# Two chunks of a normalised input, transposed by DMA on ScalarE's queue instead of by TensorE

## The chip, the cores and the metric

One Trainium2 chip; the kernel runs on one core. The metric is the device time in microseconds of one execution, lower is better. Each version is run several times and the median is taken; one further execution is profiled, and its trace gives the durations below.

## The reference

A layer normalisation of `x` (2048 rows of 1024) feeds two branches that are multiplied: a sliding, dilated attention (32 heads of 32, 8 keys at a stride of 2) and a gated MLP of width 3584. Everything is bfloat16 at the surface.

```python
xn  = layernorm(x)                           # over the 1024 columns
qkv = xn @ wqkv                              # 1024 -> 3 x 1024
o   = softmax(q . k[pos - 2*w], w = 0..7) v  # keys before row 0 masked
s   = o @ wo
g   = silu((silu(xn @ w1) * (xn @ w3)) @ w2)
out = x + s * g
```

## The kernel before, in words

**Tiling.** The 2048 rows are four chunks of 512 (`CH`), worked through as two blocks (`b` = 0, 1) of two chunks each; a chunk is four blocks of 128 rows (`NST`). The products with `wqkv`, `w1`, `w3`, `w2` and `wo` are done by a Strassen-like scheme with seven instead of eight half products: sums of weights and of activations are formed on VectorE (DVE), and TensorE multiplies them.

**What is transposed.** TensorE needs `xn` with its 1024 columns on the partitions. `xT` holds two chunks in that form (`half` = chunk mod 2, eight column groups of 128). For every 128-row block, `ln_tp` (L420) does it on TensorE: eight matmuls with the identity (L429) into two PSUM banks, and two ScalarE copies (L436) from there to `xT`. Chunks 0 and 1 are done at the start. Chunks 2 and 3 are done in `mlp_down(0)`, the second matrix product of the MLP for block 0.

**The stage around the change.** `mlp_down` runs seven products for each of four row groups `g`, one product being 14 matmuls of 128x512: w (0,0), w (1,0), T2, T1, w (1,1), T3, T4 in this order. Their right sides are loaded by SP in two halves of 896 KB each, from the weight (`w`) or from prepared sums in DRAM (`t_dram`). The left side of T1 is a sum `s1` which VectorE has put into `xT`'s memory, since the old `xT` is not needed any more; so a row group's part of `xT` comes free as its T1 product ends (cells `s1_cells`, `xt_cells`). During the first products the new x of chunks 2 and 3 is loaded into two buffers of the pool `r8` (r_5 and r_0 in the trace's numbering) and normalised in place on ScalarE (`ln_act`; its last step is L416, done before 297 us).

The T1 product goes to the banks `de`; ScalarE copies them to float32 tiles (`dsp`), and the w (1,1) product then goes on in the same banks. VectorE adds T3 and the `dsp` copies (`dsa`), and ScalarE makes the SiLUs (`gsilu`). In T3 and T4 each row group starts with an `ln_tp` of one block of chunk 2 or 3.

**What follows.** `wo(0)`, with loads of `wo` (two halves of 1 MB) and of `x` through SP; then block 1, whose attention of chunk 1 (`attention(1)`, on VectorE) and q, k, v products read `xT` and the sums `xs` of it (`xn_sums`: xs0, xs1, xs2, and later xs3).

**Order.** Nothing is issued directly: `plan.op` records every operation with what it reads and writes, a cost, and for transfers a size. TensorE's order is that of the program. For the other four engines a small simulation (`simulate`) picks, whenever an engine is free, the ready operation with the earliest due time. So a changed operation can shift the order on VectorE, ScalarE, SP and GpSimd, and the choice of buffers. All operations of one kind are emitted from one line: L307 matmuls, L316 VectorE's tensor operations, L321 ScalarE copies, L324 SiLUs, L330 DMA issues.

Of the kernel before, what the change touches and what calls it, by code (L numbers as in the profile page):

```python
# [14 lines left out]
PE, DVE, ACT, POOL, SP = range(5)  # L15
# [184 lines left out]
def kernel(  # L200
# [11 lines left out]
    nc = tc.nc  # L212
    P = 128
# [45 lines left out]
    xT = const.tile([P, 2, KT, CH], BF16, name="xT")  # L259
# [5 lines left out]
    plan = Plan()  # L265
# [13 lines left out]
        out=ident[:], in_=ident[:], compare_op=ALU.not_equal, fill=1.0,  # L279
# [4 lines left out]
        out=maskb[0:32], in_=maskb[0:32], compare_op=ALU.is_ge, fill=-1.0e9,  # L284
# [12 lines left out]
    def bank(name):  # L297
        return plan.slot("mm", name)
# [15 lines left out]
    def tt(name, fn, o, a, b, rd, wr, n, fast, late=0.0):  # L314
        occ = n / (1920.0 if fast else 960.0) + 0.068
        plan.op(DVE, name, lambda: fn(out=o(), in0=a(), in1=b()), rd, wr, occ, 0.08, late=late)  # L316
# [19 lines left out]
    def xt_cells(half, kh, st=None):  # L336
        return [("xT", half, (kh * KH + k) * 2 + q // 2, q % 2) for k in range(KH)
                for q in (range(4) if st is None else [st])]
# [17 lines left out]
    def f32(s):  # L356
        return s.ap()
# [17 lines left out]
    def xrow(xt, st):  # L375
        return xt.ap().rearrange("p (s d) -> p s d", s=NST)[:, st, :]
# [43 lines left out]
    def ln_tp(c, st, xt, engs=(ACT, ACT)):  # L420
        half = c % 2
        for kh in range(2):
            eng = engs[kh]
            tp = bank(f"tp{c}_{st}_{kh}")

            def emit(kh=kh, tp=tp):
                for k in range(KH):
                    kt = kh * KH + k
                    nc.tensor.matmul(  # L429
                        tp.ap()[:, k * P:(k + 1) * P], lhsT=xrow(xt, st)[:, kt * P:(kt + 1) * P], rhs=ident[:],  # L430
                        start=(k == 0), stop=(k == KH - 1), skip_group_check=True,
                    )

            plan.op(PE, f"tp{c}_{st}", emit, [(xt, st)], [tp], KH * TP, 0.0)
            fn = nc.scalar.copy if eng == ACT else nc.vector.tensor_copy
            plan.op(eng, f"xT{c}_{st}_{kh}", lambda kh=kh, tp=tp, fn=fn: fn(  # L436
                out=xT[:, half, kh * KH:(kh + 1) * KH, st * P:(st + 1) * P],
                in_=tp.ap().rearrange("p (k t) -> p k t", k=KH)),
                [tp], xt_cells(half, kh, st), 0.48 if eng == ACT else 0.6, 0.11, late=-1.5 if c == 1 else 0.0)


    def qkv_load(t):
# [400 lines left out]
    def gsilu(c, dh, g, src, rd, occ):  # L843
        dst, wr = gate(c, dh, g)
        silu("dg", dst, src, rd, wr, occ)

    def mlp_down(b):
# [20 lines left out]
        def prod(ps, g, row, fh, rhs, first, dt):  # L868
            src = h_sb if dt == BF16 else h16
            for q, (wt, ops) in enumerate(rhs):  # L870
                fs = range(fh * FH + q * NQ, fh * FH + (q + 1) * NQ)
                mm(ps, [lambda f=f: src[:, f, gs[row][g]] for f in fs], ops, first and q == 0,
                   [wt] + h_cells(fs, row, [g]), last=q == 1)
# [9 lines left out]
        xn = []  # L883
        for c in range(2 * b + 2, 2 * b + 4 if b + 1 < NB else 0):
            xt = plan.slot("r8", f"x{c}")
# [43 lines left out]
        rhs = rhs_load("t", t=T3)  # L929
        for g in G:  # L930
            if b + 1 < NB:
                ln_tp(2 * b + 2, g, xn[0])
            prod(pb[g], g, 1, 0, rhs, False, FP16)
            tt("dsa", add, lambda g=g: f32(sp5[g]), pb[g].ap, lambda g=g: f32(sp5[g]), [pb[g], sp5[g]], [sp5[g]], 512, False)
            gsilu(2 * b + 1, 1, g, lambda g=g: f32(sp5[g]), [sp5[g]], 0.54)
        rhs = rhs_load("t", t=T4)
        for g in G:
            if b + 1 < NB:
                ln_tp(2 * b + 3, g, xn[1])
            prod(pb[g], g, 1, 1, rhs, False, BF16)  # L940
            gsilu(2 * b + 1, 0, g, pb[g].ap, [pb[g]], 0.48)

# [142 lines left out]
    def rows0(st):  # L1085
        if st == 0:
            for q in range(2):
                ln_tp(0, q, x0)
        elif st < NST - 1:
            ln_tp(0, st + 1, x0, (ACT, ACT))  # L1090

    plan.shift = 0.0
    for b in range(NB):
# [50 lines left out]
        for fb in range(FB):  # L1144
            up_step(b, fb)
        attention(c0)
        mlp_down(b)
        wots = wo_load()
        wo_sums(wots)
# [35 lines left out]
```

## Time and profile before

| | us |
|---|---|
| median of 3 runs (lowest to highest) | 728.78 (727.29 to 729.50) |
| the profiled execution | 729.82 |
| its span | 728.1 |
| TensorE busy | 716.1 |
| VectorE busy | 643.0 |
| ScalarE busy | 394.4 |
| identity matmuls (L429), 128 in all | 219 ns median each, overlapping; 64 of them at 319 to 344 us |
| granted TensorE clock, mean | 0.995 of full |

The span is the time from the first to the last instruction on the core; the profiled execution's own time has some 1.7 us around it. Busy times of different engines overlap. Matmuls are pipelined, so the durations of single ones overlap too; the chain of work that ended last gives each piece without overlap. `mm`, `r`, `k`, `a` in the profile's rows are the pools of PSUM banks, of 8 KB buffers, of float32 tiles and of attention tiles.

### The profile page before, as it was taken

What the parts mean: (1) busy time and instruction counts of PE and PEld (TensorE: products, weight loads), DVE (VectorE), ACT (ScalarE), POOL (GpSimd) and SP (SyncE); (2) the same over time, 40 slices, a digit from 0 to 9 for tenths busy, and PEclk for the clock granted to TensorE, in tenths of its full rate; (3) what the DMA queues carried; (4) which work ended last, traced back from release to release, by engine and by line L of the source; (5) the groups of instructions that cost most, each with busy time, mean ns of one, the idle gap of its engine ahead of it and who ended that gap; (6) DMA issues with size and microseconds to landing.
All of it is one profiled execution on the core that took longest, in us unless ns stands there. A gap on an engine that the chain in (4) does not pass through costs nothing.

```text
span 728.1 us, 9409 instructions
## 1 busy us (share of the span) xinstructions
PE 716.1 (98%) x3436; PEld 348.4 (48%) x3436; DVE 643.0 (88%) x860; ACT 394.4 (54%) x672; POOL 50.0 (7%) x102
## 2 busy tenths in 40 slices
PE   7999999999999999999999999999999999999997
PEld 5555544444444444445455554444444444444443
DVE  5898999987999999764999999965999998959957
ACT  6745465657565698454444454666555654411233
POOL 0010110112000000202000000022000002020000
PEclk9999999999999999999999999999999999999999
DMA  9569886786544844477355549897537346473523
GB/s 322 199 214 382 319 298 203 256 234 224 185 170 145 302 143 162 149 212 231 117 174 174 172 150 309 280 298 238 190 115 248 117 153 210 153 252 109 174 72 102
DMA packets 120142, 148.47 MB, mean 204 GB/s; under 512 B 5408, under 2 KB 97056, under 8 KB 115744
## 3 DMA queue, kind: packets, MB, share of 16 engines
q1 hardware_dynamic: 114016, 121.65, 52.0%
q0 software_dynamic: 6080, 26.22, 9.7%
q8 instruction: 27, 0.44, 0.3%
q14 instruction: 19, 0.16, 0.1%
HBM read 106.95 MB, written 32.51 MB: 192 GB/s over the span
## 4 chain that ended last, share of the span: by engine, by line
PE 90%; DVE 5%; DMA 3%; ACT 0%; SPq 0%; issue 0%; DVEq 0%
PE mm L307 89%; DVE r L316 2%; DMA h_sb<-in_B_w_dram 2%; DMA r<-in_A_wqkv_dram 1%; DVE h_sb L316 1%; PE mm L429 1%; DVE xs L316 1%; DVE qo L316 1%; DVE small L384 0%; ACT h_sb L321 0%; SPq L330 0%; DVE r L392 0%; ACT qo L321 0%; DVE small L391 0%; DVE small L387 0%
## 5 line engine op out<-in xcount | busy, mean ns | idle before, releaser
L307 PEld LDWEIGHTS <-r 128*128 128x128 f16 (+1 forms) x2288 | 240.5, 107 | 245.3 <-DVE r L316 0.9
L307 PE MATMUL mm<-xs,r 128*128 128x512 f16 x1280 | 295.4, 379 | 0.8 <-DVE r L316 0.5
L307 PE MATMUL mm<-xT,r 128*128 128x512 bf16 (+1 forms) x1008 | 228.3, 371 | 0.5 <-DMA r<-in_A_wqkv_dram 0.5
L321 ACT COPY k<-mm 128x512 f32<-128x512 f32 x192 | 112.2, 586 | 88.2 <-PE mm L307 85.4
L307 PE MATMUL mm<-r,h_sb 128*128 128x512 bf16 (+1 forms) x704 | 154.9, 379 | 0.0
L307 PEld LDWEIGHTS <-h_sb 128*128 128x128 f16 (+1 forms) x800 | 77.9, 98 | 92.5
L321 ACT COPY mm<-mm 128x512 f32<-128x512 f32 x88 | 50.3, 573 | 83.9 <-PE mm L307 69.9
L316 DVE TENSOR_TENSOR a<-a,a 128x2048 bf16<-128x2048 bf16 (+1 forms) x72 | 87.7, 1218 | 1.3 <-DMA a<-E 0.9
L316 DVE TENSOR_TENSOR a<-qo,kT 128x2048 bf16<-128x2048 bf16 x64 | 76.8, 1217 | 0.0
L316 DVE TENSOR_TENSOR k<-mm,k 128x512 f32<-128x512 f32 x72 | 47.9, 684 | 22.0 <-PE mm L307 21.6
L316 DVE TENSOR_TENSOR a<-E,vT 128x2048 bf16<-128x2048 bf16 x56 | 66.4, 1217 | 0.0
L316 DVE TENSOR_TENSOR h_sb<-mm,k 128x512 bf16<-128x512 f32 x96 | 63.1, 683 | 1.1 <-PE mm L307 0.7
L316 DVE TENSOR_TENSOR r<-r,r 128x1024 f16<-128x1024 bf16 (+4 forms) x66 | 52.3, 798 | 7.9 <-DMA r<-in_A_wqkv_dram 5.9
L324 ACT ACTIVATE k<-k 128x512 bf16<-128x512 f32 x56 | 34.8, 631 | 44.3 <-DVE k L316 44.2
L324 ACT ACTIVATE h_sb<-mm 128x512 bf16<-128x512 f32 x60 | 35.8, 598 | 20.5 <-PE mm L307 20.4
L316 DVE TENSOR_TENSOR a<-a 128x1024 bf16<-128x1024 bf16 (+4 forms) x60 | 37.9, 632 | 9.0 <-DMA a<-E 8.0
L316 DVE TENSOR_TENSOR h_sb<-h_sb,k 128x1024 bf16<-128x1024 bf16 x56 | 36.8, 684 | 9.2 <-ACT k L321 9.0
L316 DVE TENSOR_TENSOR qo<-qo,a 128x2048 bf16<-128x2048 bf16 x32 | 39.0, 1217 | 0.0
L321 ACT CAST k<-mm 128x512 bf16<-128x512 f32 x56 | 32.6, 586 | 11.5 <-PE mm L307 11.5
L330 POOL DMA_DIRECT2D a<-E x32 | 16.6, 525 | 321.7 <-ACT k L321 138.9
L316 DVE TENSOR_TENSOR h_sb<-h_sb 128x512 f16<-128x512 bf16 (+1 forms) x72 | 37.5, 567 | 0.8 <-PE mm L307 0.6
L316 DVE TENSOR_TENSOR r<-r 128x1024 f16<-128x1024 bf16 (+1 forms) x34 | 25.7, 776 | 0.0
(75 smaller groups left out, 408.5 us busy)
## 6 DMA issues: line engine op xcount, KB each, us to landing
r<-in_B_w_dram SPq DMA_DIRECT2D x42, 512.0 KB, 4.3
s_dram<-r POOLq DMA_DIRECT2D x14, 1024.0 KB, 5.6
r<-t_dram SPq DMA_DIRECT2D x16, 896.0 KB, 6.3
r<-s_dram SPq DMA_DIRECT2D x14, 1024.0 KB, 6.1
r<-in_A_wqkv_dram SPq DMA_DIRECT2D x12, 1024.0 KB, 7.4
r<-in_B_w_dram SPq DMA_DIRECT2D x12, 896.0 KB, 5.1
h_sb<-in_B_w_dram SPq DMA_DIRECT2D x14, 512.0 KB, 10.2
t_dram<-h_sb POOLq DMA_DIRECT2D x14, 512.0 KB, 6.9
```

The source lines that it names most:

```text
L307: nc.tensor.matmul(cut(ps.ap()), lhsT=lhs[k](), rhs=cut(rhs[k]()), start=(first and k == 0), stop=(last and k == n - 1), skip_group_check= ...
L316: plan.op(DVE, name, lambda: fn(out=o(), in0=a(), in1=b()), rd, wr, occ, 0.08, late=late)
L321: plan.op(ACT, name, lambda: nc.scalar.copy(out=o(), in_=a()), rd, wr, occ, 0.11)
L324: plan.op(ACT, name, lambda: nc.scalar.activation(out=o(), in_=a(), func=ACTF.Silu), rd, wr, occ, 0.11, table="silu")
L330: plan.op(eng, name, lambda: e.dma_start(out=o(), in_=a()), rd, wr, occ, 0.0, nbytes=kb * 1024, late=late)
L429: nc.tensor.matmul(tp.ap()[:, k * P:(k + 1) * P], lhsT=xrow(xt, st)[:, kt * P:(kt + 1) * P], rhs=ident[:], start=(k == 0), stop=(k == KH - ...
```

## The change

In `mlp_down(0)`, the eight calls of `ln_tp` for chunks 2 and 3 become calls of a new function `ln_turn`. It records one transfer on ScalarE's queue for each block of 128 rows: from the normalised rows (128 x 1024, bfloat16, 256 KB) straight to the block's place in `xT` (128 x 8 x 128), transposed by the DMA. Chunks 0 and 1 stay on `ln_tp`. The planner is told 1.5 us of ScalarE and 256 KB for each.

```diff
+    def ln_turn(c, st, xt):
+
+        half = c % 2
+        plan.op(ACT, f"turn{c}_{st}", lambda: nc.scalar.dma_start(
+            out=xT[:, half, :, st * P:(st + 1) * P], in_=xrow(xt, st), transpose=True),
+            [(xt, st)], xt_cells(half, 0, st) + xt_cells(half, 1, st), 1.5, 0.0, nbytes=256 * 1024)
...
         rhs = rhs_load("t", t=T3)
         for g in G:
             if b + 1 < NB:
-                ln_tp(2 * b + 2, g, xn[0])
+                ln_turn(2 * b + 2, g, xn[0])
             prod(pb[g], g, 1, 0, rhs, False, FP16)
...
         rhs = rhs_load("t", t=T4)
         for g in G:
             if b + 1 < NB:
-                ln_tp(2 * b + 3, g, xn[1])
+                ln_turn(2 * b + 3, g, xn[1])
             prod(pb[g], g, 1, 1, rhs, False, BF16)
```

In the program that the planner makes of it, the transfers stand on ScalarE behind the `dsp` copies, two after each of the four, as soon as `xT` comes free; xs0, xs1 and xs2 stand between the `dsa` sums on VectorE; and the first load of `wo`, which reuses the buffer of chunk 2, stands ahead of T4's loads on SP.

## The prediction

> **What bounds the kernel now.** I read the page first: busy time and the chain that ended last.
>
> ```profile
> PE 716.1 (98%) x3436; PEld 348.4 (48%) x3436; DVE 643.0 (88%) x860; ACT 394.4 (54%) x672; POOL 50.0 (7%) x102
> PE 90%; DVE 5%; DMA 3%; ACT 0%; SPq 0%; issue 0%; DVEq 0%
> ```
>
> TensorE sets the end. The chain in order of time shows whether the removed work lies on it:
>
> ```profile
> 319.60 0.45 PE mm L429 x8
> 320.04 3.02 PE mm L307 x14
> ...
> 343.88 0.45 PE mm L429 x8
> 344.32 35.84 PE mm L307 x166
> ```
>
> Each group of eight L429 transposes is a piece of the chain between two products of 14 matmuls. Next, TensorE's timeline over the products around the change (each of four groups: the one on T1, a w product into the same banks, T3; T4 follows):
>
> ```profile
> 295.26 12.25 PE L307 MATMUL mm<-r,xT 128*128 128x512 f16 x56
> 307.35 12.25 PE L307 MATMUL mm<-r,h_sb 128*128 128x512 bf16 x56
> 319.43 0.61 PE L429 MATMUL mm<-ident,r 128*128 128x128 bf16 x8
> 319.88 3.19 PE L307 MATMUL mm<-r,h_sb 128*128 128x512 f16 x14
> ```
>
> There is no gap, so every load and copy is in time there. Whether it stays so depends on ScalarE, where the transfers go, and on SP's queue:
>
> ```profile
> 298.48 0.59 ACT L321 COPY k<-mm 128x512 f32<-128x512 f32 x1 [1.86 <-PE mm L307]
> 301.50 0.59 ACT L321 COPY k<-mm 128x512 f32<-128x512 f32 x1
> 304.53 0.58 ACT L321 COPY k<-mm 128x512 f32<-128x512 f32 x1 [2.44 <-PE mm L307]
> 307.55 0.58 ACT L321 COPY k<-mm 128x512 f32<-128x512 f32 x1 [2.44 <-PE mm L307]
> ```
>
> ```profile
> 306.79 0.53 SPq L330 DMA_DIRECT2D r<-t_dram  x1
> 307.37 1.88 SPq L330 DMA_DIRECT2D a<-E  x3
> 309.34 0.53 SPq L330 DMA_DIRECT2D r<-t_dram  x1
> 318.12 1.88 SPq L330 DMA_DIRECT2D r<-t_dram  x2
> ```
>
> The four copies are `dsp`, one for each T1 product; the waits of 2.44 us between them are free ScalarE time. The two single `t_dram` loads are T3's halves, the pair at 318.12 is T4's. The DMA view for 299 to 317 us (40 slices of 0.45 us, busy tenths) and three of its landing rows:
>
> ```profile
> DMA  9999640000000055576589899999999999999830
> r<-t_dram SPq DMA_DIRECT2D x2, 896.0 KB, 7.4
> out_dram<-r SPq DMA_DIRECT2D x12, 256.0 KB, 2.3
> r<-in_A_x_dram SPq DMA_DIRECT2D x16, 256.0 KB, 5.3
> ```
>
> The engines fill up when T3's loads start and fall empty at about 316.2: there T3's data has landed.
>
> **What goes away.** Eight groups on the chain, 8 x 0.45 = 3.60 us of TensorE. Sixteen ScalarE copies (L436; pairs of 1.07, so 16 x 0.53 = 8.5 us) go too; ScalarE is off the chain and waits 1.6 to 1.9 us before most pairs, so that is worth nothing.
>
> **What comes in: ScalarE's issue time.** The changed program's order puts two transfers behind each `dsp` copy. The copies must be read before the second w product adds to the same bank: it starts at 307.35 and goes on by 3.02, so `dsp` 1, 2 and 3 must end by 310.4, 313.4 and 316.4. A transposing issue is in no row here. The nearest rows are SP's plain issues, 0.36 (`t_dram`) to 0.94 us (half of the pair's 1.88). I take 0.94, since the new form is the harder one, and keep an upper end open for a rival. Then the first pair leaves by 299.07 + 1.88 = 300.95, before `dsp` 1 at 301.50; the same holds for the later pairs: all eight fit in the 2.44 us gaps. `dsp` is not delayed; price nothing. Behind the last pair at about 310.0 wait the SiLUs (first at 311.36), the kT halo copy and the softmax exponential (323.07); none is late.
>
> **What comes in: waits between the queues.** In the built program, ScalarE's transfers take turns with SP's on eight completion semaphores, and each transfer waits for the one before on its semaphore. The wait lists give: T3's first half waits for the third transpose in order of issue, an `a<-E` transfer ahead of T3's second half waits for the fifth (first of chunk 3), T4's first half waits for the seventh, the second `wo` load for the eighth, and the sixth and seventh transposes themselves, on ScalarE, wait for the second and fourth. The first `wo` load, which overwrites chunk 2, moves ahead of T4's loads. T3's second half is the tightest: product T3 now begins at 319.43, and needs it after seven matmuls of 0.216, at 320.94. The fifth transpose leaves at 304.53 + 0.58 + 0.94 = 306.05. Landing: 2.3 us (`out`, 256 KB) to 5.3 us (`x`, 256 KB). I take 5.3, as this window is busy: 311.4. One 0.6 us issue and T3's load of 7.4 us give 319.4; at 2.3 us it is not later than today's 309.34. Spare: 1.5 us at worst. T3's first half: third transpose leaves at 302.1 + 0.94, lands by 308.4, load by 315.8, wanted at 319.43. T4, wanted at 331.5: seventh leaves at 309.1, lands by 314.4; T4's issue is held by TensorE until 318 anyway. Price nothing, with 1.5 us the margin.
>
> **What comes in: bytes.** 8 x 256 KB = 2.1 MB; at the 310 GB/s that the slices hold while full, 6.8 us of all 16 engines. The slices before 309 us leave 5.4 us free. The remaining 1.4 us push T3's landing from 316.2 to 317.6, still early. The far end: q1's 114,016 packets took 52% of 16 x 728.1 us, 53 ns each; a transfer cut into 1,024 pieces of 256 bytes is then 3.4 us, eight 27 us; in pieces of 32 bytes eight times that. I take the copy's speed, the rows of equal size.
>
> **DVE.** xs0, xs2 and xs1 (1.14 us each) move from 346.9-351.5 to between the T3 sums, where DVE waits up to 2.78 us at a time; they need all eight transposes, wanted near 326, landed by 316. T3 and T4 end earlier, so `wo`'s second load (9.5 us to landing, DVE's 6.74 us wait) is issued 1.8 us earlier. Together DVE is 3.4 + 1.8 us ahead, more than the 3.6 TensorE gains, so the next point at which TensorE waits for it (0.47 us at 384.08) comes no worse. What is late next is T3's second half.
>
> **Sum.** 729.82 (profiled: span 728.1 and 1.7 around it) - 3.60 = 726.2. The three runs' median, 728.78, is 1.0 below that execution, so I give 728.78 - 3.60 = 725.2. A measurement of this kernel tells 0.3% (2.2 us) from no change.
>
> **Rivals.** *The transfers are slow and TensorE waits for T3 (slower).* For it: no row shows a transpose by DMA, and queues couple. At 3.4 us each the fifth lands at 300 + 17 = 317, T3's half at 325, a wait of 4 us; queued behind everything (27 us and the 10 that these slices hold already, from 299) it would be 336, a wait of 15. Net +0.5 to +11.4, middle +6: 735. It decides from where the fifth lands after 312.9, about 2.6 us each, and loses the whole gain at 3.3. The Trainium skill speaks for it: VectorE: DVE Perf Modes, "The three transpose paths", gives a 128x128 transpose 390 ns on TensorE and 1309 ns by DMA, and says to use TensorE where PSUM will do. By that eight blocks, if one after another, are an estimated 10.5 us a transfer, and the time near 775; the row here is 0.45 us for eight blocks on TensorE, and no row shows the DMA.
>
> *The issue is long and ScalarE holds its copies (slower).* At 4 us each `dsp` 2 ends at 299.07 + 16.6 + 0.6 = 316.3 (wanted 313.4) and `dsp` 3 at 324.9: TensorE stands 8.4 us, and T3's load, behind the fifth transpose, makes it 1.2 to 4.2 more: net +6 to +9, near 736. With the tightest sum above it breaks even between 2.2 and 2.8 us, by the landing. Against it: plain issues of up to 1,024 pieces take 0.94. The Trainium skill's DMA: Bandwidth & Descriptors, in the table behind "Why a DMA increments its semaphore by 16 and not by 1", gives earlier generations 32 cycles of the issuing sequencer per tile of a transpose within SBUF; with its 512 cycles for a plain issue beside 0.366 us here, an estimated 1.5 us for 64 tiles, 2.9 for 128. By 1.5 the sum holds, by 2.9 it lies between +0.5 and +3.5.
>
> *The gain is eaten:* issues of about 2 us or landings some microseconds over 5.3 give 727 to 730. That the transposes stay on TensorE is excluded: its program has 64 matmuls fewer.
>
> **Numbers.** Forecast 0.45 (alone 724 to 727), eaten 0.12, long issue 0.23, slow transfers 0.20. So faster 0.45, same 0.12, slower 0.43. The range takes in the forecast, the eaten gain, the long issue and the nearer half of the slow transfers: 724 to 741.
>
> **What would show it.** Right: L429 gone from 319-344, the products touching, the first T3 matmul near 319.4, `dsp` copies at today's times, T3's second load issued before 313. Wrong: TensorE idle before T3 with a DMA as releaser (slow transfers), before the second w product with ScalarE as releaser (long issue), or DVE waiting at xs for transposes after 330.

## The result, and the profile after

| | us |
|---|---|
| median before (5 runs, lowest to highest) | 728.78 (727.28 to 729.54) |
| median after (5 runs, lowest to highest) | 731.90 (729.63 to 732.78) |
| ratio after / before | 1.0039 (95% interval 1.0023 to 1.0055) |
| profiled execution after, its span | 731.11, 729.3 |

The change made the kernel slower by 3.1 us; 3.6 us less had been forecast. The profiled executions differ by less, 731.11 against 729.82, because the one of before lies 1.0 above its median and the one of after 0.8 below. So the rows below account for the 1.3 us between these two executions and show by which mechanism the sign turned.

The traces here reach the start of the T1 products between 292.2 and 295.5 us. The three whose granted clock does not fall to half in the first 20 us (e1, e3 and e7 below) come at 292.2 to 293.0, the others at 293.9 to 295.5. So stages are compared from that start on (first row of the third fence below).

The page of after: the 64 identity matmuls are gone (3436 became 3372 instructions), TensorE is less busy, and yet the span is longer.

```profile
PE 714.7 (98%) x3372; PEld 345.1 (47%) x3372; DVE 642.6 (88%) x860; ACT 388.0 (53%) x656; POOL 50.0 (7%) x102
```

The chain in order of time (start, duration, what) now leaves TensorE. It goes through an attention transfer `a<-E` on SP and then through T3's second load:

```profile
306.09 8.29 DMA a<-E
...
314.44 10.42 DMA r<-t_dram
...
324.90 395.62 PE mm L307 x1825
```

TensorE's timeline (start, duration, what, and in brackets the idle time before the row with what ended it):

```profile
295.09 12.25 PE L307 MATMUL mm<-r,xT 128*128 128x512 f16 x56
307.17 12.25 PE L307 MATMUL mm<-r,h_sb 128*128 128x512 bf16 x56
320.19 1.67 PE L307 MATMUL mm<-r,h_sb 128*128 128x512 f16 x7 [0.77 <-DMA r<-t_dram]
324.90 24.37 PE L307 MATMUL mm<-r,h_sb 128*128 128x512 f16 x105 [3.04 <-DMA r<-t_dram]
349.11 1.89 PE L307 MATMUL mm<-r,qo 128*128 128x512 bf16 x8
```

T3 waits 0.77 us for its first half and 3.04 us for its second. The 105 matmuls that follow take 24.37 us; the same 105 take 22.82 us where nothing disturbs them (second row of `e2_plain_copy`, below). The table by stretch says why (start and end, length, then busy time of PE, PEld, DVE, ACT and POOL with their counts, then the granted clock, DMA share and GB/s): after the wait the clock falls to half for some 3 us.

```profile
324.00:326.00 2.00, 1.10 (x3) 0.41 (x3) 0.76 (x1) 0.00 (x0) 0.00 (x0) 0.66 1.12 196
326.00:328.00 2.00, 2.00 (x6) 0.75 (x5) 0.46 (x1) 0.00 (x0) 0.00 (x0) 0.50 1.10 351
328.00:330.00 2.00, 2.00 (x11) 0.88 (x9) 1.77 (x4) 1.10 (x2) 0.00 (x0) 0.98 1.08 346
```

ScalarE's timeline shows the `dsp` copies and behind each a pair of transposing transfers:

```profile
298.31 0.59 ACT L321 COPY k<-mm 128x512 f32<-128x512 f32 x1 [1.87 <-PE mm L307]
298.37 3.31 ACTq L444 DMA_TRANSPOSE xT<-r  x2
301.72 0.58 ACT L321 COPY k<-mm 128x512 f32<-128x512 f32 x1 [2.82 <-PE mm L307]
301.74 2.71 ACTq L444 DMA_TRANSPOSE xT<-r  x2
304.49 0.58 ACT L321 COPY k<-mm 128x512 f32<-128x512 f32 x1 [2.19 <-PE mm L307]
304.57 3.57 ACTq L444 DMA_TRANSPOSE xT<-r  x2
308.19 0.58 ACT L321 COPY k<-mm 128x512 f32<-128x512 f32 x1 [3.11 <-PE mm L307]
308.21 10.55 ACTq L444 DMA_TRANSPOSE xT<-r  x2
318.81 0.63 ACT L324 ACTIVATE h_sb<-k 128x512 bf16<-128x512 f32 x1 [10.04 <-issue]
```

The copies begin within 0.7 us of their old times. The last pair is another matter: its two issues take 4.74 and 5.72 us and hold ScalarE, so the first SiLU, which stood at 311.36 before, begins at 318.81. No wait of TensorE in these rows is put down to it. SP's queue shows T3's two loads, which stood at 306.79 and 309.34 before:

```profile
307.46 0.72 SPq L330 DMA_DIRECT2D r<-t_dram  x1
308.23 5.02 SPq L330 DMA_DIRECT2D a<-E  x3
314.44 0.37 SPq L330 DMA_DIRECT2D r<-t_dram  x1
```

Last, the DMA view for 299 to 317 us: the free slices of before (digits 0 from 302 to 305 us) are filled, and q10, the transposes, alone takes 61% of the engines' time. The shares of the queues add up to over 100%, since packets of different queues overlap on an engine. T3's halves now take 12.7 and 10.4 us to land (6.3 and 8.6 before), and even the 64 KB `a<-E` transfers 8.3 instead of 4.4.

```profile
DMA  9999969989999998999999899989997999999999
q10 hardware_dynamic: 6384, 1.59, 61.4%
r<-t_dram SPq DMA_DIRECT2D x2, 896.0 KB, 11.6
a<-E SPq DMA_DIRECT2D x8, 64.0 KB, 8.3
```

The account, up to the first `wo` product: -3.60 (identity matmuls) + 0.77 + 3.04 (waits) + 1.55 (105 matmuls at 24.37 instead of 22.82) = +1.8; that product starts at 349.11 instead of 347.18, +1.9, and counted from the start of T1 +2.1. (The products overlap: 12.25 us long, they follow each other every 12.08. So each of the two waits costs some 0.17 us more than the idle time in brackets.) Behind it, before's wait of 0.47 us at 384.08 is gone.

**Measures used below.** "Stage" is the time from the start of T1 to a product well into block 1's q, k, v (the fifth run of 16 matmuls on `xs`, at 420.37 before): 125.11 us before, 126.54 after. "Piece" is the time of one packet of q10 (some 256 bytes) on its engine: q10's share, times the window, times 16 engines, over its packets; after, in 299 to 339 us, 36.4% x 40 us x 16 / 8,448 = 27.6 ns (e9, whose transfers go out later: 322 to 350 us). Since packets overlap on an engine, a piece's time beside other transfers holds waiting too.

### The profile page after: what moved, and what is told of

Its sections match the earlier page's. It is cut to its first block, busy times and chain, and to the rows that moved or that the text cites. A ratio compares the mean times of both kernels' runs of the same rounds, so it can differ in the third digit from the quotient of the medians.

```text
span 729.3 us, 9290 instructions
## 1 busy us (share of the span) xinstructions
PE 714.7 (98%) x3372; PEld 345.1 (47%) x3372; DVE 642.6 (88%) x860; ACT 388.0 (53%) x656; POOL 50.0 (7%) x102
## 3 DMA queue, kind: packets, MB, share of 16 engines
q10 hardware_dynamic: 8448, 2.10, 2.0%
## 4 chain that ended last, share of the span: by engine, by line
PE 80%; DVE 14%; DMA 3%; issue 1%; ACT 0%; SPq 0%; DVEq 0%
PE mm L307 80%; DVE a L316 6%; DVE h_sb L316 3%; DVE r L316 2%; DMA r<-t_dram 1%; DMA a<-E 1%; DVE qo L316 1%; DMA r<-in_A_x_dram 1%; DVE k L316 1%; DVE small L384 1%; DVE xT L316 1%; PE mm L429 0%; DVE E L316 0%; SPq L330 0%; DVE r L392 0%
## 5 line engine op out<-in xcount | busy, mean ns | idle before, releaser
L324 ACT ACTIVATE k<-k 128x512 bf16<-128x512 f32 x56 | 34.8, 631 | 36.4 <-DVE k L316 36.4
L324 ACT ACTIVATE h_sb<-mm 128x512 bf16<-128x512 f32 x60 | 35.8, 598 | 22.1 <-PE mm L307 22.0
## 6 DMA issues: line engine op xcount, KB each, us to landing
h_sb<-in_B_w_dram SPq DMA_DIRECT2D x14, 512.0 KB, 10.5
```

What stands on the lines that cost most here:

```text
L324: plan.op(ACT, name, lambda: nc.scalar.activation(out=o(), in_=a(), func=ACTF.Silu), rd, wr, occ, 0.11, table="silu")
```

## The experiments

TensorE waits for T3's loads. Four causes were to be told apart: 2.1 MB in small pieces fill the DMA engines; SP's queue is held by semaphores that it shares with the transfers; the transposition itself is slow; ScalarE's issues are long. Each expectation says which of them is its theory and which its rival. The kernel before was run again beside each kernel (medians 728.9 to 729.0).

| kernel | median us | ratio to before, 95% interval | stage us | piece ns |
|---|---|---|---|---|
| the change | 731.90 | 1.0039 (1.0023 to 1.0055) | 126.54 | 27.6 |
| e1_no_turn | 724.94 | 0.9940 (0.9925 to 0.9956) | 120.86 | none |
| e5_eighth_of_bytes | 724.92 | 0.9946 (0.9932 to 0.9960) | 120.86 | 26.0 |
| e2_plain_copy | 726.25 | 0.9965 (0.9951 to 0.9978) | 121.81 | 22.5 |
| e3_lists_on_gpsimd | 729.21 | 1.0016 (0.9998 to 1.0034) | 125.80 | 23.8 |
| e6_chunk2_only | 728.50 | 0.9997 (0.9986 to 1.0008) | 124.12 | 21.8 |
| e7_chunk3_only | 731.19 | 1.0033 (1.0018 to 1.0049) | 127.72 | 31.4 |
| e4_chunk3_later | 725.78 | 0.9961 (0.9948 to 0.9975) | 121.99 | 22.1 |
| e10_chunk3_after_first_t3 | 724.64 | 0.9948 (0.9932 to 0.9965) | 120.86 | 25.9 |
| e9_both_later | 735.25 | 1.0096 (1.0071 to 1.0121) | 128.21 | 25.8 |
| e8_filled_wait | 730.23 | 1.0023 (1.0004 to 1.0043) | 128.07 | 29.0 |

### The ceiling, and the bytes: e1_no_turn and e5_eighth_of_bytes

```diff
 # e1_no_turn
-        plan.op(ACT, f"turn{c}_{st}", lambda: nc.scalar.dma_start(
-            out=xT[:, half, :, st * P:(st + 1) * P], in_=xrow(xt, st), transpose=True),
+        plan.op(ACT, f"turn{c}_{st}", lambda: None,
 # e5_eighth_of_bytes
-            out=xT[:, half, :, st * P:(st + 1) * P], in_=xrow(xt, st), transpose=True),
+            out=xT[:, half, 0, st * P:(st + 1) * P], in_=xrow(xt, st)[:, 0:P], transpose=True),
```

Expected of e1_no_turn:

> Leaves out the transposing of chunks 2 and 3 altogether: the eight operations keep their places in the planner, but nothing is issued, so xT holds old data. Theory (T3's loads come late behind and beside the transposes): with no transposes T3's second load is issued near 309 us again, TensorE does not wait before or in T3, the clock stays full, and the time is 728.8 - 3.6 = 725.2, about 6.5 us under the changed kernel. Rival (the order that the planner made, on VectorE and SP, costs the time by itself): 728 or more, with a wait of TensorE elsewhere.

Expected of e5_eighth_of_bytes:

> Each of the eight transposes moves only the first of its eight 128x128 blocks (32 KB instead of 256 KB), so most of xT stays old; their number, places, and the kind of waits stay. Theory (the engines' time for 2.1 MB in 256-byte pieces makes T3's loads late): T3's second load issued near 310, landed by 318, no wait of TensorE, full clock, 725 to 725.5. Rival (the transposing issues and the waits between the queues cost it whatever the size): a wait of 2 us or more stays, 729 to 731.

Both came out as the theory says, with the same stage of 120.86 us, 4.25 us below before's. In e1 TensorE goes from the w product through T3 and T4 without a gap, at full clock:

```profile
304.31 36.42 PE L307 MATMUL mm<-r,h_sb 128*128 128x512 bf16 x166
```

In e5 the number of transfers, their queue and their waits stay, only the bytes fall to an eighth; ScalarE's and the DMA view's rows:

```profile
300.47 2.40 ACTq L444 DMA_TRANSPOSE xT<-r  x2
q10 hardware_dynamic: 1280, 0.26, 5.2%
```

So neither eight transfers on ScalarE nor their semaphores cost TensorE anything by themselves; the bytes bring the loss. The issue of a pair still takes 2.4 us: it hardly depends on the size.

### The transposition: e2_plain_copy

```diff
-            out=xT[:, half, :, st * P:(st + 1) * P], in_=xrow(xt, st), transpose=True),
+            out=xT[:, half, :, st * P:(st + 1) * P], in_=xrow(xt, st).rearrange("p (k t) -> p k t", k=KT)),
```

> The same eight transfers from the same rows to the same places, 256 KB each in pieces of 256 bytes, but as plain copies without the transpose (xT's contents are not transposed). T3's second load still waits for the fifth transfer. Theory that a transposing transfer itself is slow (27.6 ns per piece and engine, 14.6 us of all 16 engines for the eight): plain copies take about half, the fifth lands before 312, T3's second load lands by 321, TensorE waits under 1 us: 725 to 726.5. Rival that any 2 MB in this window do it: fifth transfer near 314, TensorE waits 3 us or more, 730 to 732.

```profile
307.47 13.76 PE L307 MATMUL mm<-r,h_sb 128*128 128x512 bf16 x61
322.02 22.82 PE L307 MATMUL mm<-r,h_sb 128*128 128x512 f16 x105 [0.79 <-DMA r<-t_dram]
```

```profile
q10 hardware_dynamic: 8320, 2.10, 29.2%
r<-t_dram SPq DMA_DIRECT2D x4, 896.0 KB, 10.2
xT<-r ACTq DMA_DIRECT2D x8, 256.0 KB, 5.1
```

A copy of the same pieces without transposition takes 22.5 ns a piece, 8,320 x 22.5 ns / 16 = 11.7 us of all engines, 180 GB/s. That is less than the change's 27.6 ns, but not the half that the theory had named. Its forecast came true all the same: 726.25 us, and T3 waits only 0.79 us. The rival, that any 2 MB in this window do it, fell. So small pieces are not the whole cause: the same pieces as plain copies cost a fifth of the wait (0.79 of 0.77 + 3.04 us).

Where the transfers are alone on the engines, the two kinds are equal: from 302 to 305 us q10 moves 2,575 packets in after and 2,471 here (214 and 208 GB/s), and e4's below take 22.1 ns. Beside other transfers they are not. The stretch from 307 to 313 us before, after and here, with the DMA share and GB/s at the end:

```profile
307.00:313.00 6.00, 6.00 (x30) 2.70 (x29) 1.92 (x2) 1.22 (x2) 1.70 (x4) 1.00 0.96 259
307.00:313.00 6.00, 6.00 (x29) 2.69 (x28) 0.69 (x1) 0.58 (x1) 1.51 (x3) 1.00 1.16 143
307.00:313.00 6.00, 5.95 (x28) 2.74 (x28) 1.30 (x2) 0.59 (x2) 1.82 (x4) 1.00 1.10 233
```

The engines are full in all three. q10 moves 0.33 MB of this in after and 0.35 MB here, but everything else 0.53 against 1.05 MB: beside other transfers the transposing ones hold these up more than plain copies do. The same six us, counted from T1, show 155 GB/s in e7 and 123 in e8; in e3, with all `a<-E` transfers on GpSimd's queue, they show 223, and the next six 170. A second difference is in the same experiment. The first three pairs of plain copies are issued in 1.4 to 1.8 us instead of 2.7 to 3.6 and the last in 3.0 instead of 10.6, so they start sooner. How much of the 5.65 us between the two medians belongs to which was not tried alone.

The Trainium skill, Advanced Engine Details and Errata, "X-Bar Transpose (TRN2)", says that transposing transfers are as fast as regular ones, and expects 350 to 400 GB/s. The first holds here against copies in equal pieces where they are alone; at the second the runs show 189 GB/s (e4, 327 to 331 us) to 224 GB/s (e4, 302 to 305 us).

### The queues' coupling: e3_lists_on_gpsimd

```diff
-                dma((POOL, SP)[sq % 2], f"L{c}", lambda r=r, sq=sq: Lv(r // 2)[sq * 32:(sq + 1) * 32, r % 2],
+                dma(POOL if c == 1 else (POOL, SP)[sq % 2], f"L{c}", lambda r=r, sq=sq: Lv(r // 2)[sq * 32:(sq + 1) * 32, r % 2],
```

> The changed kernel with the eight a<-E transfers of chunk 1's attention that SP issues moved to GpSimd's queue, so that none stands ahead of T3's second load with a wait for the fifth transpose. Theory that the wait for the semaphore carries most of it: second load issued by 310, landed by 321, TensorE waits under 1.5 us: 725.5 to 727. Rival that the 16 DMA engines are simply full from 299 us on: the load is issued early and lands no sooner (323 or later), 730 to 732.

With the `a<-E` transfers off SP, both T3 loads are issued at once (T1 starts 2.1 us earlier than in after, so this is 305.9 on its scale; the second load goes out some 7 us sooner), and T3's second half waits as long as ever:

```profile
303.79 1.88 SPq L330 DMA_DIRECT2D r<-t_dram  x2
```

```profile
322.00 24.46 PE L307 MATMUL mm<-r,h_sb 128*128 128x512 f16 x105 [3.14 <-DMA r<-t_dram]
```

The two loads landed 10.0 and 16.7 us after their issue. So the late issue was a consequence: the semaphore that held it waited for an `a<-E` transfer that was itself slow in the full engines. My theory had given the coupling most of the loss and fell. The rival, full engines, holds in its mechanism, though the median of 729.21 lies below its 730 to 732. About 0.7 us of the wait (3.81 to 3.14) may be the coupling's, and the stages differ by as much. The medians of the change and of e3 differ by 2.7 us, with intervals that overlap; what makes the rest stays open.

### The place: e6_chunk2_only, e7_chunk3_only, e4_chunk3_later

```diff
 # e6_chunk2_only: the fourth chunk back on TensorE
-                ln_turn(2 * b + 3, g, xn[1])
+                ln_tp(2 * b + 3, g, xn[1])
 # e7_chunk3_only: the third chunk back on TensorE
-                ln_turn(2 * b + 2, g, xn[0])
+                ln_tp(2 * b + 2, g, xn[0])
 # e4_chunk3_later: prod marks T3 products; the fourth chunk's transfers read the mark of the second
-            prod(pb[g], g, 1, 0, rhs, False, FP16)
+            prod(pb[g], g, 1, 0, rhs, False, FP16, mark=[("t3", g)])
...
-                ln_turn(2 * b + 3, g, xn[1])
+                ln_turn(2 * b + 3, g, xn[1], [("t3", 1)])
```

In the names, "chunk2" and "chunk3" count from 0: the third and the fourth chunk.

> Only chunk 2 by DMA, chunk 3 by TensorE and copies as before. Theory: four transposes (298 to 306 us, when the engines had 3 us free) delay T3's loads by under 2 us, inside their spare time; TensorE saves 4 x 0.45 = 1.8 us and does not wait: 727.0. Rival (any transposes in front of T3's loads cost more than they save): 728.5 or more.

> Only chunk 3 by DMA, at its place in the changed kernel (from 304.5 us, together with T3's loads); chunk 2 by TensorE. Theory (it is the time shared with T3's loads that counts): T3's second load lands 4 to 6 us later than before, near 320 to 321, TensorE waits 0 to 1.5 us of it: 727 to 728.5. Rival (the number of bytes alone counts): as chunk 2 alone, 727.0.

> The changed kernel with chunk 3's four transposes made to follow the second T3 product (about 326 us), when T3's loads and T4's have landed; chunk 2's stay at 298 to 306. Theory (bytes and waits in front of T3): T3's loads see only half of the transposes, most of them before the loads start, TensorE waits under 1 us, and the time is 725 to 726.5. Rival (the DMA time only moves: wo, x and the E transfers at 330 to 345 come late instead, or VectorE waits for xs): 727 to 731 with a wait of TensorE at 344 to 360.

e6 and e7 move the same 1.05 MB. The third chunk's, issued at 298.8 to 305 us into half-empty engines, cost 21.8 ns a piece and T3 nothing; e7's, which went out at 301.5 to 315 beside T3's loads (304.8 to 318.5 on the scale of e6, since T1 starts 3.3 us earlier in e7), 31.4 ns a piece and a wait of 2.79 us, with the clock again at 0.50 behind it:

```profile
321.27 3.03 PE L307 MATMUL mm<-r,h_sb 128*128 128x512 f16 x7 [2.79 <-DMA r<-t_dram]
```

In e6 half the identity groups are gone, but only 1.0 us of the 1.8 arrives: TensorE waits for VectorE 1.27 us where before it waited 0.47. VectorE's sums of the new `xT` still wait for the fourth chunk's copies (1.41 us, until 343.48); that this makes the later wait is likely, but not shown.

```profile
383.33 3.65 PE L307 MATMUL mm<-xs,r 128*128 128x512 f16 x16 [1.27 <-DVE r L316]
```

The theory's 727.0 for e6 was missed by 1.5 us. The time is the rival's (728.5 or more), but not its mechanism, since T3 does not wait. e7 came out above what either side expected. e4 keeps all eight transfers and puts the fourth chunk's behind T3's loads, into the engines' emptier time at 325 us:

```profile
325.21 1.25 ACTq L444 DMA_TRANSPOSE xT<-r  x1
326.55 4.08 ACTq L444 DMA_TRANSPOSE xT<-r  x3
```

```profile
307.59 36.42 PE L307 MATMUL mm<-r,h_sb 128*128 128x512 bf16 x166
```

```profile
q10 hardware_dynamic: 8448, 2.10, 29.2%
r<-t_dram SPq DMA_DIRECT2D x4, 896.0 KB, 6.4
xT<-r ACTq DMA_TRANSPOSE x8, 3.4
```

No wait in T3, full clock, loads back at 6.4 us and the transposes at 3.4: 3.2 us faster than before, with the same bytes. Two waits for VectorE remain (0.30 and 0.45 us).

### How far the place goes: e10_chunk3_after_first_t3 and e9_both_later

```diff
 # e10_chunk3_after_first_t3: as e4, with the mark of the first T3 product
-                ln_turn(2 * b + 3, g, xn[1], [("t3", 1)])
+                ln_turn(2 * b + 3, g, xn[1], [("t3", 0)])
 # e9_both_later: as e4, and the third chunk there too
-                ln_turn(2 * b + 2, g, xn[0])
...
+                ln_turn(2 * b + 2, g, xn[0], [("t3", 1)])
                 ln_turn(2 * b + 3, g, xn[1], [("t3", 1)])
```

> The third chunk's transfers as in the changed kernel, the fourth chunk's after the first product of T3 instead of the second, 1.9 us earlier than in e4_chunk3_later. Theory: T3's loads have landed or are about to; no wait of TensorE in T3, and the copies of the fourth chunk are ready earlier, so that the two short waits of e4 (0.30 and 0.45 us) shrink: 725 to 726.5. Rival (even the tail of T3's second load is held up by them): a wait of 1 us or more in T3, 726.5 to 728.

> All eight transfers wait for the second product of T3, so that none lies beside T3's loads and all lie beside the loads of T4 and wo. Theory (the small pieces only hurt where they lie beside a load that is wanted within about 15 us): T3 goes without a wait; eight transfers take some 12 to 14 us of the DMA engines from about 325 us on, where the third chunk's blocks are now wanted by the copies at 332 to 345; 726 to 728, with waits of TensorE for VectorE or for a load of 1 to 3 us near 345 to 385 us. Rival (the bytes cost the same wherever they lie): a wait of 3 us or more for T4's or wo's load, 729 to 731.

e10 has the lowest median of all, 724.64, 0.9948 of before and just under its forecast of 725 to 726.5, and its stage is e1's to the hundredth: the transposes cost TensorE nothing. Its chain has TensorE without a break from 27.1 to 671.8 us:

```profile
27.13 644.63 PE mm L307 x2986
```

In e9, T3 is as undisturbed as in e4, and the kernel is slower than with the change, well beyond what either side expected. TensorE's timeline:

```profile
343.62 1.89 PE L307 MATMUL mm<-r,qo 128*128 128x512 bf16 x8
349.27 1.89 PE L307 MATMUL mm<-h_sb 128*128 128x512 f16 x8 [3.76 <-DVE h_sb L316]
...
363.02 1.92 PE L307 MATMUL mm<-xs,r 128*128 128x512 f16 x8 [3.15 <-DVE r L316]
```

and VectorE's, where the sums of `wo` wait for its load (its second half landed 13.1 us after its issue, 10.1 before and 6.9 in e4):

```profile
347.99 1.22 DVE L316 TENSOR_TENSOR h_sb<-r,r 128x2048 f16<-128x2048 bf16 x1 [13.04 <-DMA r<-in_A_wo_dram]
```

The same 2.1 MB beside T3's loads cost T3, beside `wo`'s they cost `wo`; split between the two empty stretches they are free.

### The slow matmuls: e8_filled_wait

Fourteen matmuls into a bank that nobody reads stand between the halves of the first T3 product, to keep TensorE at work in the wait.

```diff
+                if idle and q == 0:
+                    wb = bank("keepwarm")
+                    for r_ in range(2):
+                        mm(wb, [lambda f=f: src[:, f, gs[row][g]] for f in fs], ops, r_ == 0,
+                           [wt] + h_cells(fs, row, [g]), last=r_ == 1)
...
-            prod(pb[g], g, 1, 0, rhs, False, FP16)
+            prod(pb[g], g, 1, 0, rhs, False, FP16, idle=b == 0 and g == 0)
```

> The changed kernel with 14 matmuls of no use (3.02 us, into a free bank, from operands that are there) between the first and the second half of the first T3 product, where TensorE waited 3.04 us; the planner is told that they take no time. Theory (the wait is the DMA's, and the idle time behind it halves the granted clock for 3 us, another 1.7 us): T3's second half starts at about the same time, at full clock, and the time falls by some 1.7 us to 730.2. Rival (the slow matmuls after the wait come of something else, such as the busy DMA): the matmuls stay slow, 731.5 to 732.

```profile
321.90 4.69 PE L307 MATMUL mm<-r,h_sb 128*128 128x512 f16 x21 [2.76 <-DMA r<-t_dram]
327.69 22.82 PE L307 MATMUL mm<-r,h_sb 128*128 128x512 f16 x105 [1.09 <-DMA r<-t_dram]
```

The median is as expected, 730.2. In the profiled execution the 105 matmuls take 22.82 us with the DMA engines as full as in after (share 1.09 from 328 to 331 us; after, 1.10 from 326 to 328), so full engines alone do not slow matmuls. But the loads came later in this execution, the filler did not stand in the longer wait, and the clock stayed at 1.00 behind 2.76 us of idleness too. So that the filler saved the clock is not shown by this profile, and the intervals of e8 and of the change overlap: the agreement of the median may be chance.

## Why the prediction was wrong, by its steps

**The step that failed is the term of the bytes.** It took the rate of copies in large pieces, 310 GB/s and 6.8 us of all engines, as "the rows of equal size", and let T3's data land at 317.6. T3's second half landed at 324.86. The runs show 11.7 us for these pieces, transposed in e4 where most of them are alone and as plain copies in e2 (22.1 and 22.5 ns each), and 14.6 us in the change (8,448 x 27.6 ns / 16). And they show what the term had no place for: beside the `a<-E` transfers and T3's loads the transposing ones hold up the rest, with 143 GB/s in all from 307 to 313 us where before had 259.

The term also began from a landing of T3 at 316.2, where the slices fall empty; the landing row of the second half gives 309.34 + 8.6 = 317.9. With 317.9 and 11.7 in its own arithmetic, and its 5.4 us free before 309, T3's second half lands at 317.9 + 11.7 - 5.4 = 324.2. Wanted was 320.94. That this comes so near to the measured 324.86 is partly luck: the same sum stands for e2, whose second half starts at 322.02 already, and 14.6 us would give 327.1. So the way was right and the sizes were not. The far end, 53 ns a piece and 27 us, was above the truth; the value lay between the two ends and I took the near one by size in KB, where the size of a piece should have chosen the row.

**The tightest sum** ("spare 1.5 us at worst") inherits this: T3's load was to land 7.4 us after its issue, the median of both halves, where the second's own was 8.6; it took 10.4, and its issue, allowed until 313, was at 314.44. The couplings were read rightly in kind, but what came last at SP was an `a<-E` transfer of SP's own, slowed by the full engines; in e3's profile the coupling is worth some 0.7 us by itself.

**Missing from the sum** was what a wait of TensorE does to the clock: 1.55 us more, half of the second half's wait again.

**ScalarE's issue time** was put at 0.94 us and is 1.3 at the least, 1.6 in the median and 5.72 at the most. The first three pairs overran their gaps by up to 0.7 us, and no `dsp` copy was late for its bank, so the rival of the long issue did not occur. But "none is late" failed behind the last pair: the first SiLU was 7.5 us late, at no cost to TensorE that these rows show. The estimate of 1.5 us for 64 tiles, from the table of the Trainium skill's DMA: Bandwidth & Descriptors behind "Why a DMA increments its semaphore by 16 and not by 1", comes near the median, but not by its rule of a time per tile: an eighth of the data took 1.11 to 1.39 us.

**The rival of slow transfers** was the mechanism, with a chance of 0.20: TensorE waits for T3, the gain is lost, and the net lies at the low end of its +0.5 to +11.4. Its own price, 3.4 us a transfer one after another, was too high for the transfer alone (3.2 to 4.4 us to land in e4, with several under way at once). The Trainium skill's 1309 ns for a 128x128 block (VectorE: DVE Perf Modes, "The three transpose paths"), by which the prediction estimated 10.5 us a transfer, does not add up block by block here: in e4 a transfer of eight blocks lands in about a third of that.

**What held:** the eight groups are worth 3.6 us on the chain, the `dsp` copies stay, VectorE comes no worse, and without the full engines the gain arrives, 4.0 us in e1 and 4.3 in e10 against 3.6 forecast. The measured 731.9 lies in the range of 724 to 741, in the part that the rivals added.

## What to carry to other kernels

Price a transfer by its pieces, not by its bytes: take the time of a packet from a queue with pieces of the same size. For a transposing transfer a plain copy in equal pieces gives its time where it is alone (e2 and e4), but not what it does to loads beside it (233 against 143 GB/s). Here the transfers that replaced work of the bounding engine were free only where the DMA engines were empty; look at the slices for the next load that is wanted, and put the transfer behind it by a dependence, as e10 does, rather than where its buffer comes free. A wait of TensorE of about 3 us may cost its length and half of it again, by the clock (after, e3 and e7), or its length alone (e9).

## What the runs showed of the hardware

- A transposing transfer within SBUF and a plain one in pieces of 256 bytes cost the same where they are alone: 214 and 208 GB/s (after and e2, 302 to 305 us). Beside `a<-E` and T3's loads the rest gets half as much through with the transposing ones (0.53 against 1.05 MB from 307 to 313 us), and over a whole run a transposed piece takes 24 to 31 ns (e3, after, e7) and a plain one 22.5 (e2).
- The issue of a transposing transfer on ScalarE takes 1.2 to 1.9 us for 256 KB (e4) and 1.1 to 1.4 us for 32 KB (e5). In the full engines single ones took up to 5.7 us (after) and 7.3 us (e7), and ScalarE did nothing else meanwhile; the issue of a plain copy took 0.60 to 0.84 us there (e2).
- The clock was at 0.50 after idle times of TensorE of 2.79 us (e7), 3.04 (after) and 3.14 us (e3), and at 1.00 after 2.76 (e8) and after 3.76 and 3.15 us (e9). So the length alone does not decide. The changes of the clock lie whole multiples of 3.41 us apart (half from 10.62 to 14.04 and from 324.65 to 328.06 us in after). On this grid, carried on from the half clock at the start of a run where there is no other, TensorE was busy for 0.63 (after), 0.34 (e3) and 0.62 us (e7) of the stretch before a drop. In the emptiest stretches around the waits of e8 and e9, with no drop behind them, it was busy for 1.41 and 1.45 us: these waits of 2.76, 3.76 and 3.15 us lie across two stretches each. The first row is of after, ahead of the drop at 324.65; the other two are of e8:

```profile
321.24:324.65 3.41, 0.63 (x3) 0.20 (x2) 1.99 (x3) 1.23 (x2) 0.00 (x0) 1.00 1.22 300
317.73:321.14 3.41, 1.41 (x7) 0.54 (x6) 0.49 (x1) 1.35 (x3) 0.00 (x0) 1.00 1.06 207
321.14:324.55 3.41, 2.65 (x13) 1.23 (x13) 2.01 (x3) 0.15 (x1) 0.00 (x0) 1.00 1.21 191
```

- The Trainium skill, TensorE: Matmul & The Clock Gate, "Part 1: The HAM clock gate", gives half the clock after an idle window of about 3.4 us whose phase is free. The halving, the 3.41 us and the free phase agree; the stretches ahead of the drops were not wholly idle. How much work in a stretch keeps the clock stays open: at the start of before, among smaller matmuls, a drop follows a stretch with 1.72 us of it (7.92 to 11.33 us).
